# A long convolution by FFT on one core: last stage by row groups in turn, sixteen spectrum buffers, other DRAM copies

## The chip, the core and the metric

The kernel runs on one core of one Trainium2 chip. A core has five engines with their own instruction streams: TensorE (PE in the profile; its weight loads are shown as PEld), VectorE (DVE), ScalarE (ACT), GpSimd (POOL) and SyncE (SP), which here only issues DMAs. They wait for each other through semaphores. The metric is the device time of one execution in microseconds, lower is better. The kernel before was timed three times: 247.57, 248.12 and 249.15 us, median 248.12.

## The reference

Inputs are bf16: `A_u` [1, 2048, 512], parameters of a state-space layer of 512 channels with 128 complex states each, and a small feed-forward network of width 1376.

```python
xn = layernorm(A_u)
K  = real(sum_n C * exp(dt*A*l) * dt*B)            # [512, 2048], one kernel per channel
s  = irfft(rfft(xn padded) * rfft(K padded))[:2048] + xn * Dskip
r  = xn @ B_w_r                                    # one score for each row
i  = argmax(r)                                     # a single row is selected
upd = zero except row i: (silu(xn_i @ w_gate) * (xn_i @ w_up)) @ w_down * sigmoid(r_i)
g  = silu(xn + upd)
out = A_u + s * g
```

So there is one causal convolution of length 2048 in each of 512 channels, whose kernel K must first be generated, and a gate that needs a feed-forward network for one row alone.

## The kernel before

**Where the order comes from.** The Python code records every operation with the buffers that it reads and writes (`_Graph.op`). `schedule` takes a table `ORDER`, written out as numbers of operations, one list for each engine, and `emit` puts each engine's operations out in that order, with the waits that the recorded reads and writes ask for. Each engine is strictly in order; an operation that waits holds up all that follows on its engine, and a DMA that waits holds up SP. Many operations go through helpers, so the profile shows the helper's line: `tt` (two tensors, DVE) is L592, `ts` L599, `cp` L602, `act` L586, `evac` (out of PSUM) L620 on ACT or L621 on DVE, `evac_a` L624, `mm` L641, `dma` L658. Groups are told apart by their buffers.

**The stages, in the order of the data.**

1. Load and layer norm: `X0` to `XN` (bf16, [4 column groups q, 2, 16 rows b, 64]); row l = 16p + b lies on partition p. XN is moved to `XZN` by 16 DMAs, four of its rows to `X4`, and it is stored to DRAM twice, as `scr_x` and `scr_g`, by one DMA of 2 MB each.
2. Router and feed-forward network: a score for each row (`JNK`, L785), argmax through small PE and DVE steps, weights through a ring of eight buffers `WRING` of which five lie where XN was. The result is a row `GRW`, which POOL scatters into `scr_g` at the place that `SMI` names.
3. `useq`, `useq2`: the forward transform of xn, PE `CB,XZN` to `AU` and `AU,F2U` to `UST`, stored as `scr_u` (eight stores).
4. The kernel generator, once for each half h of the channels: exponentials `E` on ACT (`exps`), a chain of complex products on DVE for `GG` (`kgen_g`, buffers TT, MB) and `Q` (`kgen_q`), then 512 small matmuls `QQ,GG` (`kgen_mm`: eight operations of 64) whose results `KE` are sorted by `kx` into `KX[h]`. GG and E are single buffers, used by both halves.
5. `spec(h)`: 16 positions kp, each 10 matmuls `KX,FD` of 128x256 into bank 5 or 6, evicted to a buffer `KF`, which DVE multiplies into `UU[h]` (the product U*KF). `FD` (5 MB) comes in four loads into the space of AU. `UU[0]` lies where the first half's Q was, the first part of `UU[1]` where MB was, its second part where the second half's Q was; each is 4 MB and read back from `scr_u` by `load_u`, in two portions of positions.
6. `inv_a(h)`: 16 operations of eight matmuls `CB,UU`, evicted to `C`. Each needs all 16 products of that half.
7. `fpre`: on DVE and ACT, XNR = xn * Dskip * silu(gate) and XR = A_u + XNR, where XNR is read back from `scr_x`, the gate G0 from `scr_g`, XR from A_u.
8. `fin`, the last stage: 512 matmuls `C,FB`, each 32x32 weights with 128 columns, tile position (32q, 32a). Four blocks bb of four rows for each of the 16 row classes a; a block has four PSUM banks, one for each q. A block's operations are one for each q: 32 matmuls, all in row group q, the column group a running fastest. In block 3 a matmul `VM,CB` (with E127, four partitions) first puts a correction into each bank. Evictions: q even by ACT, then a product with G0 on DVE; q odd by a DVE product straight out of PSUM; then a sum into XR and stores to `out`.

In the table of before, PE has spec0 spread between the second half's QQ,GG operations, its kx1 and, at the end, spec1 with inv0; only three KF buffers serve both halves in turn. The last stage's operations for different q stand one after another.

Of the kernel before, what the change touches and what calls it, by code (L numbers as in the profile page):

```python
# [7 lines left out]
ACT = mybir.ActivationFunctionType  # L8
# [8 lines left out]
KB = 1024  # L17
# [323 lines left out]
def tables():  # L341
# [16 lines left out]
    for l in range(2044):  # L358
# [18 lines left out]
        7 223 8 16 3 9 225 221 12-13 15 17 14 174 110-111 109 107-108 104-106 175 173 167-168 166 169-170 172 171 179 176 178 177 233 231 235 227 229  # L377
        237 239 241 243 245 247 249 251 259 261 263 265 267 269 271 273 343 350 694 357 364 695 275 277 279 371 378 287 700 699 698 385 696-697 392
        784 787 703 702 701 882 789 785 879 786 788 878 871 876-877 880 870 883 881 873-875 872 921-922 920 923 940-941 939 938 956-959 978-979
        982-983""",  # L380
    scalar="""
        2 4 6 10 5 11 18-19 21 20 22-23 28 30 29 31 43 482 468 476 466 477 471 393 474 492 485 26 484 472 496 486 490 473 475 45 487 495 479 489 494
        470 480 491 478 95 465 467 35 469 483 493 394 464 156 481 395 47 443 433 444 396 451 449 437 457 460 434 397 448 436 459 399 458 442 452-453
        456 435 407 462 49 439 406 404 461 441 412 432 446 398 445 290-291 417 413 297 296 293-294 419 418 299-300 302-303 424 306 309 416 311 438 308
        422 312 282 425 463 314-315 317-318 321 320 323-324 440 450 330 326-327 329 455 454 332-333 335-336 526 341-342 447 338-339 537 348 346 345
        349 353 355-356 352 362 257 360 363 359 549 606 609 600 547 366-367 578 607 553 369 373 597 604 596 374 581 595 370 582 594 377 376 605 599
        593 590 598 584 603 583 608 592 580 591 561 588-589 602 579 587 577 586 559 585 383-384 567 380-381 569 388 390-391 575 387 565 563 573 571
        650 640 708 705 711 714 720 668 717 670 726 723 674 732 678 680 682 692 688 738 741 747 750 755 800 803 753 757 806 809 897 885 889 827 893
        765 775 836 773 779 783 839 843 847 853 851 857 855 861 859 865 863 869 867 915 910 933 928 951 946 973 968 981 980 984-985""",
    vector="""  # L390
        1 220 0 54-57 64 114 113 65 112 115 63 51 123 27 25 52-53 117 24 60 59 120 119 61 118 121 50 116 58 62 126 66 124-125 68 67 122 70 69 127 89
        128 71 93 130 72 34 94 33 32 36 132 129 91 39 131 151 133 90 134 150 135 155 136 37 137 154 138 40 86 92 87-88 139 102 97 140 101 103 100 141
        98 152 181 142 99 143 96 183 144 38 145 180 146 185 147 182 148 41 149 153 187 157 401 161 163 165 162 405 159-160 164 158 403 184 189 400 186
        191 188 498 193 409 408 190 195 192 414 194 411 196 497 197 402 198 415 200 420 202 500 499 203 501 204 410 205 502 421 207 503 305 209 505
        211 504 210 212 423 506-507 426 509 508 429 511 214 510 427 219 513 512 428 515 514 283 517 516 284 519 518 529 520-521 528 523 527 522 530
        525 531 524 254 533 532 536 253 535 256 534 255 539 258 541 538 540 542-543 639 545 544 551 611 610 649 613 557 555 281 651 641 285-286 614
        612 616 615 618 617 620 619 621-626 576 627-630 632 631 642 634 633 644 636 635 706 637-638 643 712 646 645 652 648 647 654 653 664 656 655
        709 657-658 721 660 659 666 662 661 718 715 672 727 724 733 676 729 684 730 686 693 690 901 735 904 736 905 739 903 902 742 744-745 748 751
        791 794-795 792 797-798 801 804 759 807 810 763 812-813 815-816 767 818 821 819 822 824 761 825 828 830 771 831 833-834 769 837 777 781 841
        845 849 888 884 890 886 891 887 892 896 894 916 911 895 917 912 898 918 934 919 935 913 929 914 930-931 936 932 937 952 949 947 953 948 950  # L400
        954 971 955 899 969 972 970 974 976 975 977""",
    gpsimd="""
        431 488 430 73-85 601 288""",
    tensor="""
        42 44 46 48 289 295 292 199 201 298 301 206 304 208 307 310 213 313 316 215-218 319 322 222 224 226 328 325 228 230 232 234 331 334 236 238
# [4 lines left out]
        944 943 960 964 963 967 945 961 965""",  # L410
# [7 lines left out]
def build(nc, A_u, A_A_re, A_A_im, A_B_re, A_B_im, A_C_re, A_C_im, A_log_dt, A_Dskip,  # L418
# [22 lines left out]
    p_ = np.arange(128)  # L441
    lidxb = 128.0 * p_[:, None] + np.arange(16)[None, :] + 16384.0
# [6 lines left out]
    cf_list = [("PRMF", perm), ("ONES", ones), ("LIDX", lidxb), ("MISC", misc)]  # L449
# [18 lines left out]
    SCRX = nc.dram_tensor("scr_x", [128 * 8192], BF16)  # L468
    SCRG = nc.dram_tensor("scr_g", [128 * 8192], BF16)

    with g.ctx:
# [76 lines left out]
        XNR = g.buf("XNR", RA, [4, 2, 16, 64], BF16)  # L548
# [13 lines left out]
        KF = [g.buf(f"KF{i}", RT + 9 * KB + 1024 * i, [4, 128], BF16) for i in range(3)]  # L562
# [5 lines left out]
        TB = [g.buf(f"TB{i}", RG + 16 * KB + 1024 * i, [512], BF16) for i in range(3)]  # L568
        V4 = g.buf("V4", RG + 19 * KB, [512], BF16)
# [244 lines left out]
        tt(DV, sml(8, 0, 8), sml(5, 0, 8), CF(CF.a[m0 + 1:m0 + 2], 0, 8), ALU.add)  # L814
# [37 lines left out]
        for fc in range(11):  # L852
# [18 lines left out]
             r=[GRW(None, 0, 8), SMI(None, 0, 8)], cost=1400, dma=16 * KB, tokr=["scrg"], tokw=["row"])  # L871
# [204 lines left out]
        def load_u(h, c):  # L1076
            g.stage = f"ldu{h}"
            uu = UU[h]
            toks = [f"scru{kp}" for kp in range(4 * c, 4 * c + 4)]
            base = 8192 * h + 16 * c * 64  # L1080
            for p0, s0, n in ((0, 0, 128), (0, 64, 64), (64, 0, 64)):
                g.stage = f"ldu{h}" if n == 128 else f"ldv{h}"
                dst = uu(uu.a[0 if n == 128 else 1][:, 16 * c:16 * c + 16].reshape(4, 1024), p0, n)
                load(dst, dram(SCRU, s0 * 16384 + base, [[16384, n], [2048, 4], [1, 1024]]), n * 8192, tokr=toks)
# [164 lines left out]
```

## Time and profile before

| | |
|---|---|
| median of three runs | 248.12 us |
| the profiled execution: its own time | 246.94 us |
| its span, first to last instruction | 244.9 us |
| mean granted TensorE clock | 0.826 |
| busy: PE, DVE, ACT, POOL | 169.0, 194.8, 139.8, 8.2 us |
| DMA moved | 43.27 MB, mean 177 GB/s |
| `C,FB` matmuls (last stage) | 512, 211.5 to 236.7 us |
| `CB,UU` matmuls (inv_a) | 256, 170.2 to 210.5 us |

The profile gives, for one execution, the busy time of each engine, the span cut into 40 slices of 6.1 us (one digit of tenths each), the chain of work that ended last (followed back from the last instruction through what released each step), groups of instructions, and DMA issues. "issue" in the chain is time in which an engine waited for nothing that the profile shows. Durations of matmuls hold their pipeline latency, so a count of starts in a stretch says more of the pace than a mean duration does. On DVE and ACT an instruction starts some 0.08 us before the one ahead of it is recorded as ended; "net" below is a duration less this.

### The profile page before, as it was taken

What the parts mean: (1) busy time and instruction counts of PE and PEld (TensorE: products, weight loads), DVE (VectorE), ACT (ScalarE), POOL (GpSimd) and SP (SyncE); (2) the same over time, 40 slices, a digit from 0 to 9 for tenths busy, and PEclk for the clock granted to TensorE, in tenths of its full rate; (3) what the DMA queues carried; (4) which work ended last, traced back from release to release, by engine and by line L of the source; (5) the groups of instructions that cost most, each with busy time, mean ns of one, the idle gap of its engine ahead of it and who ended that gap; (6) DMA issues with size and microseconds to landing.
All of it is one profiled execution on the core that took longest, in us unless ns stands there. A gap on an engine that the chain in (4) does not pass through costs nothing.

```text
span 244.9 us, 6504 instructions
## 1 busy us (share of the span) xinstructions
PE 169.0 (69%) x2790; PEld 128.3 (52%) x2790; DVE 194.8 (80%) x399; ACT 139.8 (57%) x278; POOL 8.2 (3%) x22
## 2 busy tenths in 40 slices
PE   0330000599887669787646369999999999899970
PEld 0220000374754356655425248878999999665430
DVE  4799999998999995599999943478779649777335
ACT  2699999997997679993420014232488526410200
POOL 2008000000000000010000000000000000000000
PEclk9999999999755577996895757979999999955555
DMA  6980099991766978479989900599999940003306
GB/s 221 329 347 1 0 143 142 301 431 29 229 202 194 278 210 304 130 164 321 398 257 237 236 26 7 125 219 213 229 217 246 214 110 0 3 3 86 90 3 171
DMA packets 26204, 43.27 MB, mean 177 GB/s; under 512 B 2144, under 2 KB 18240, under 8 KB 25280
## 3 DMA queue, kind: packets, MB, share of 16 engines
q1 hardware_dynamic: 24704, 42.01, 64.2%
q10 hardware_dynamic: 1440, 0.85, 1.2%
q8 instruction: 22, 0.36, 0.6%
q14 instruction: 6, 0.05, 0.1%
q0 software_dynamic: 32, 0.00, 0.0%
HBM read 30.26 MB, written 10.49 MB: 166 GB/s over the span
## 4 chain that ended last, share of the span: by engine, by line
PE 52%; DVE 27%; ACT 7%; issue 5%; DMA 3%; POOL 2%; SPq 1%; DVEq 0%
PE PB L641 52%; DVE TT L592 6%; DVE JNK L785 4%; DVE QQ L592 3%; DMA X<-in_A_u_dram 3%; ACT AU L620 3%; DVE GG L592 3%; ACT UST L624 2%; DVE ST L735 2%; DVE XN L599 2%; POOL LST L592 2%; ACT QQ L586 1%; DVE XR L592 1%; DVE TB L592 1%; DVE SL L592 1%
## 5 line engine op out<-in xcount | busy, mean ns | idle before, releaser
L641 PE MATMUL PB<-KX,FD 128*128 128x256 bf16 x320 | 43.5, 298 | 7.9 <-ACT KF L620 6.9
L641 PEld LDWEIGHTS PB<-KX,FD 128*128 128x128 bf16 x320 | 32.8, 107 | 16.1 <-ACT KF L620 8.5
L641 PE MATMUL PB<-QQ,GG 128*20 128x42 bf16 x1024 | 25.0, 263 | 8.6 <-issue 5.5
L592 DVE TENSOR_TENSOR UU<-UU,KF 128x1024 bf16<-128x1024 bf16 x32 | 21.6, 687 | 9.9 <-ACT KF L620 9.5
L641 PEld LDWEIGHTS PB<-QQ,GG 128*20 128x20 bf16 x1024 | 21.9, 123 | 12.2 <-issue 7.3
L641 PE MATMUL PB<-CB,UU 128*128 128x128 bf16 x256 | 26.3, 255 | 0.1
L641 PEld LDWEIGHTS PB<-CB,UU 128*128 128x128 bf16 x256 | 24.9, 201 | 1.4 <-DVE C L621 0.4
L641 PE MATMUL PB<-C,FB 32*32 32x128 bf16 x512 | 23.7, 388 | 0.7 <-ACT C L620 0.7
L592 DVE TENSOR_TENSOR TT<-GG,MB 128x2048 bf16<-128x2048 bf16 (+2 forms) x24 | 23.1, 994 | 0.1
L641 PE MATMUL PB<-CB,XZN 32*128 32x64 bf16 x256 | 14.1, 327 | 13.0 <-DMA XZN<-XN 10.5
L620 ACT ACTIVATE KF<-PB 128x512 bf16<-128x512 f32 x19 | 11.1, 596 | 18.5 <-PE PB L641 13.7
L586 ACT ACTIVATE E<-AR 128x256 bf16<-128x256 f32 x64 | 21.6, 419 | 0.0
L641 PEld LDWEIGHTS PB<-CB,XZN 32*128 32x128 bf16 x256 | 12.1, 201 | 15.0 <-DMA XZN<-XN 10.7
L592 DVE TENSOR_TENSOR QQ<-QQ,E 128x1024 bf16<-128x1024 bf16 (+2 forms) x16 | 19.8, 1254 | 0.0
L620 ACT ACTIVATE C<-PB 128x512 bf16<-128x512 f32 x21 | 12.6, 598 | 12.3 <-PE PB L641 11.3
L624 ACT ACTIVATE UST<-PB 128x512 bf16<-128x512 f32 x32 | 17.3, 602 | 3.8 <-PE PB L641 3.7
L641 PEld LDWEIGHTS PB<-C,FB 32*32 32x32 bf16 x512 | 13.2, 113 | 10.6 <-issue 1.7
L641 PE MATMUL PB<-AU,F2U 64*128 64x256 bf16 x128 | 13.5, 361 | 7.0 <-ACT UST L624 3.9
L586 ACT ACTIVATE TB<-PB 128x512 bf16<-128x512 f32 x8 | 4.7, 596 | 22.7 <-PE PB L641 12.7
L620 ACT ACTIVATE AU<-PB 128x512 bf16<-128x512 f32 x31 | 16.6, 646 | 1.6 <-PE PB L641 1.6
L620 ACT ACTIVATE KE<-PB 128x336 bf16<-128x336 f32 x9 | 4.0, 449 | 22.4 <-PE PB L641 22.4
L592 DVE TENSOR_TENSOR GG<-TT 128x1024 bf16<-128x1024 bf16 (+2 forms) x28 | 14.0, 532 | 1.7 <-PE PB L641 1.5
(120 smaller groups left out, 264.5 us busy)
## 6 DMA issues: line engine op xcount, KB each, us to landing
FD<-c_fd SPq DMA_DIRECT2D x4, 1280.0 KB, 10.1
scr_u<-UST SPq DMA_DIRECT2D x8, 512.0 KB, 5.8
UU<-scr_u SPq DMA_DIRECT2D x8, 512.0 KB, 10.9
UU<-scr_u SPq DMA_DIRECT2D x4, 1024.0 KB, 9.8
X<-in_A_u_dram SPq DMA_DIRECT2D x4, 512.0 KB, 8.3
XZN<-XN SPq DMA_DIRECT2D x16, 128.0 KB, 4.0
scr_g<-XN SPq DMA_DIRECT2D x1, 2048.0 KB, 9.0
scr_x<-XN SPq DMA_DIRECT2D x1, 2048.0 KB, 13.6
```

What stands on the lines that cost most here:

```text
L586: g.op(AC, lambda e: e.activation(out=out.ap, in_=in_.ap, func=func, **kw), w=[out], r=r, cost=cost(AC, out, 0.71) + (92 if bias is not No ...
L592: g.op(eng, lambda e: e.tensor_tensor(out=out.ap, in0=a.ap, in1=b.ap, op=op), w=[out], r=[a, b], cost=cost(eng, out, rate))
L599: g.op(eng, lambda e: e.tensor_scalar(out=out.ap, in0=a.ap, scalar1=x1, scalar2=x2, op0=op0, **kw), w=[out], r=r, cost=cost(eng, out, rate))
L620: g.op(AC, lambda e: e.activation(out=out.ap, in_=in_.ap, func=ACT.Copy), w=[out], r=[in_], cost=cost(AC, out, 0.71), alt=(DV, lambda e: e ...
L624: g.op(AC, lambda e: e.activation(out=out.ap, in_=in_.ap, func=ACT.Copy), w=[out], r=[in_], cost=cost(AC, out, 0.71))
L641: ins = e.matmul(o_.ap, lhsT=l_.ap, rhs=r_.ap, start=st, stop=sp, **kw)
L735: g.op(DV, lambda e, b=b: e.bn_stats(ST6(ST6.a[b]).ap, X0(X0.a[b]).ap), w=[ST6(ST6.a[b])], r=[X0(X0.a[b])], cost=620)
L785: g.op(DV, lambda e, b=b, ro=ro, jk=jk: e.tensor_tensor_reduce(out=jk(jk.a.reshape(8, 64)).ap, in0=xb(XN, b).ap, in1=WRB(WRB.a.reshape(8, ...
```

## The change

- The last stage: one operation holds one row class b4 of a block, 32 matmuls in which the row group q runs fastest, so that neighbours differ in q; it writes four banks. The last block is cut into two of two rows. The correction matmuls are eight, of two rows each (128x256), instead of four. PSUM is evicted in pairs of q: the pair 0,1 by two ACT copies and one DVE product of 1024 elements for each partition, the pair 2,3 by two DVE products from PSUM; then one DVE sum for each pair. `TB` are four buffers of 1024 elements.
- KF: 16 buffers; spec0 uses one for each position, spec1 five of them. KF0 to KF2 lie where they were, KF3 to KF7 behind KX, KF8 to KF15 in the space of E.
- `load_u`: one load for the first part of UU[h] (all positions), two for the second, with 16 KB in one piece for each partition. All wait for all of `scr_u`.
- `scr_x` and `scr_g` are stored by four DMAs each in the row order of the last stage, and A_u is copied inside DRAM to `scr_a` in that order, so that G0, XR and XNR are read back by one, one and two loads instead of four each. The scatter index is worked out for the new order (two more DVE operations, one matmul of 128x8).
- XNR lies in two pieces, one over KE and XN, one over TT and KF0 to KF2. `fpre` works on pairs of q: 24 DVE products and sums of 1024 elements for each partition instead of 12 of 2048.

A new `ORDER` goes with it. In the new table:

- SP issues the copy to `scr_a` after the first weights and before the X4 and XZN moves; the last two FD loads come before the UU[0] loads, then stand: first part of UU[1], GRW, one half of XNR, DSK, second part of UU[1], G0, XR, FB, other half of XNR.
- PE has all 16 positions of spec0 together, ahead of the second half's QQ,GG; inv0 starts between these and kx1, spec1 comes after kx1.
- DVE evicts seven of the first half's eight KE operations (ACT did five of them before) and takes all but one of the 16 products of spec0 after the second half's Q; ACT's exponentials of the second half stand earlier, among the evictions to UST.
- In the last stage PE has: one operation of block 0, the four of block 1, then the other three of block 0 with the corrections of block 3 between them, block 3, block 2, the corrections of block 4, block 4.

The diff without the table:

```diff
+    addrb = 128.0 * (32 * (p_[:, None] % 4) + p_[:, None] // 4) + np.arange(16)[None, :]
...
+    SCRA = nc.dram_tensor("scr_a", [128 * 8192], BF16)
...
-        XNR = g.buf("XNR", RA, [4, 2, 16, 64], BF16)
+        XNR = apart("XNR", RX + 8 * KB, RT + 4 * KB, [2, 2, 16, 64])
...
-        KF = [g.buf(f"KF{i}", RT + 9 * KB + 1024 * i, [4, 128], BF16) for i in range(3)]
+        KF = [g.buf(f"KF{i}", RT + 9 * KB + 1024 * i if i < 3 else RQ0 + 37 * KB + 1024 * (i - 3) if i < 8 else RM + 1024 * i, [4, 128], BF16) for i in range(16)]
...
         for t, nm in ((SCRX, "scrx"), (SCRG, "scrg")):
-            store(t.ap().rearrange("(p f) -> p f", p=128), XN(XN.a.reshape(-1)), 128 * 16384, tokw=[nm])
+            for a in range(4):
+                dma(dram(t, 262144 * a, [[8192, 32], [1, 8192]]), bass.AP(tensor=XN.handle, offset=a * XN.row, ap=[[4 * XN.row, 32], [1, 8192]]), 32 * 16384, r=[XN(XN.a.reshape(-1))], tokw=[f"{nm}{a}"])
+        g.stage = "cpa"
+        dma(dram(SCRA, 0, [[8192, 32], [262144, 4], [1, 8192]]), _dma_rows(A_u, 0, [[32768, 32], [8192, 4], [1, 8192]]), 128 * 16384, tokw=["scra"])
...
-        tt(DV, sml(8, 0, 8), sml(5, 0, 8), CF(CF.a[m0 + 1:m0 + 2], 0, 8), ALU.add)
+        tt(DV, LST(LST.a[7]), oneh, cf("ADDR"), ALU.mult)
+        red(sml(9), LST(LST.a[7]), ALU.add)
+        mm([(mv(134, 1, 0, 8), cf("ONE8"), sml(9), True, True, None)], 300)
+        tt(DV, sml(8, 0, 8), mv(134, 1, 0, 8), CF(CF.a[m0 + 1:m0 + 2], 0, 8), ALU.add)
...
+        def load_u(h):
+            uu = UU[h]
+            toks = [f"scru{kp}" for kp in range(8)]
+            load(uu(uu.a[0].reshape(8192)), dram(SCRU, 8192 * h, [[16384, 128], [1, 8192]]), 128 * 16384, tokr=toks)
+            for i in range(2):
+                load(uu(uu.a[1].reshape(8192), 64 * i, 64), dram(SCRU, 8192 * h + (1 - i) * 64 * 16384, [[16384, 64], [1, 8192]]), 64 * 16384, tokr=toks)
...
-                kf = KF[n_ % 3]
+                kf = KF[3 + n_ % 5 if h else n_]
...
+        for qp in range(2):
+            load(XNR(XNR.a[qp].reshape(-1)), dram(SCRX, 4096 * qp, [[8192, 128], [1, 4096]]), 128 * 8192, tokr=[f"scrx{a}" for a in range(4)])
+        load(G0(G0.a.reshape(-1)), dram(SCRG, 0, [[8192, 128], [1, 8192]]), 128 * 16384, tokr=[f"scrg{a}" for a in range(4)] + ["row"])
+        load(XR(XR.a.reshape(-1)), dram(SCRA, 0, [[8192, 128], [1, 8192]]), 128 * 16384, tokr=["scra"])
...
+        for kb, (r0, nr) in enumerate(((0, 4), (4, 4), (8, 4), (12, 2), (14, 2))):
+            bk = [PB[4 * (kb % 2) + q] for q in range(4)]
+            if r0 >= 12:
                 for q in range(4):
-                    mm([(bk[q](bk[q].a.reshape(4, 128)), CB(cb("E127"), 0, 4), VM(VM.a[:, 128 * q:128 * q + 128], 0, 4), True, None, None)], 215)
-            for q in range(4):
+                    mm([(bk[q](bk[q].a[0:128 * nr].reshape(nr, 128)), CB(cb("E127"), 0, 4), VM(VM.a[r0 - 12:r0 - 12 + nr, 128 * q:128 * q + 128], 0, 4), True, None, None)], 215)
+            for b4 in range(nr):
                 lst = []
-                for b4 in range(4):
-                    for ri in range(2):
-                        for a in range(4):
-                            l1 = 16 * a + 4 * bb + b4
+                for ri in range(2):
+                    for a in range(4):
+                        l1 = 16 * a + r0 + b4
+                        for q in range(4):
                             lst.append((bk[q](bk[q].a[128 * b4:128 * b4 + 128].reshape(2, 64), 32 * a, 32), FB(FB.a[l1, ri], 32 * q, 32),
...
                 mm(lst, 28)
...
+                for q in range(2):
+                    if qp:
+                        tt(DV, t_(t_.a[128 * nr * q:128 * nr * (q + 1)].reshape(2, nr, 64)), cols(2 * qp + q), G0(G0.a[2 * qp + q, :, r0:r0 + nr]), ALU.mult)
+                    else:
+                        act(t_(t_.a[128 * nr * q:128 * nr * (q + 1)].reshape(2, nr, 64)), cols(2 * qp + q), ACT.Copy)
+                if not qp:
+                    tt(DV, tv(0, 2), tv(0, 2), gv(0, 2), ALU.mult)
+                xv = XR(XR.a[r0:r0 + nr, 256 * qp:256 * qp + 256].reshape(nr, 4, 64).transpose(1, 0, 2))
+                tt(DV, xv, t_(t_.a[0:256 * nr].reshape(4, nr, 64)), xv, ALU.add)
```

More of the change, by code (lines that the diff above doesn't have):

```diff
@@ L384 @@
[L384 to L387, printed above, removed]
@@ L411 @@
+        963-964 944-947 979 976-978 980-981""",
 )
@@ L567, in build @@
         XR = g.buf("XR", RG, [16, 512], BF16)
-        TB = [g.buf(f"TB{i}", RG + 16 * KB + 1024 * i, [512], BF16) for i in range(3)]
-        V4 = g.buf("V4", RG + 19 * KB, [512], BF16)
+        TB = [g.buf(f"TB{i}", RG + 16 * KB + 2048 * i if i < 2 else RQ0 + 33 * KB + 2048 * i, [1024], BF16) for i in range(4)]
+        V4 = g.buf("V4", RQ1 + 41 * KB, [512], BF16)
         FIX = {DV: 62.0, AC: 118.0, PO: 250.0}
@@ L870, in build @@
         g.op(PO, lambda e: e.indirect_dma_start(out=rows, out_offset=bass.IndirectOffsetOnAxis(ap=SMI(None, 0, 8).ap, axis=0), in_=GRW(None, 0, 8).ap, in_offset=None),
-             r=[GRW(None, 0, 8), SMI(None, 0, 8)], cost=1400, dma=16 * KB, tokr=["scrg"], tokw=["row"])
+             r=[GRW(None, 0, 8), SMI(None, 0, 8)], cost=1400, dma=16 * KB, tokr=[f"scrg{a}" for a in range(4)], tokw=["row"])
         g.stage = "useq"
@@ L1073, in build @@
             kgen_mm(h)
-        def load_u(h, c):
+        def load_u(h):
+            uu = UU[h]
+            toks = [f"scru{kp}" for kp in range(8)]
             g.stage = f"ldu{h}"
[L1078 to L1084, printed above, removed]
+            load(uu(uu.a[0].reshape(8192)), dram(SCRU, 8192 * h, [[16384, 128], [1, 8192]]), 128 * 16384, tokr=toks)
+            g.stage = f"ldv{h}"
+            for i in range(2):
+                load(uu(uu.a[1].reshape(8192), 64 * i, 64), dram(SCRU, 8192 * h + (1 - i) * 64 * 16384, [[16384, 64], [1, 8192]]), 64 * 16384, tokr=toks)
         def load_fd(buf, i, k0):
@@ L1196, in build @@
+            for a in range(4):
+                store(_dma_rows(out, 8192 * a + 512 * r0, [[32768, 32], [1, 512 * nr]]), XR(XR.a[r0:r0 + nr].reshape(-1), 32 * a, 32), 32 * 1024 * nr, eng=SP if r0 < 12 or a < 2 else AC)
         g.schedule(ORDER)
```

106 lines of the change are left out of this document (46 added, 60 removed), and 7 rows, old and new, of the table tensor.

## The prediction

> **What bounds the kernel now.** I read the busy slices first, then the chain that ended last in order of time, then stretches of the last third. In the slices, VectorE (DVE) is full to about slice 23 and TensorE (PE) from slice 25 on; in the last five slices the granted clock is half.
>
> ```profile
> PE   0330000599887669787646369999999999899970
> ...
> DVE  4799999998999995599999943478779649777335
> ...
> PEclk9999999999755577996895757979999999955555
> ```
>
> The chain says the same: up to 136 us DVE (the generators), then PE with small gaps, then 25.6 us of the last stage, then a tail on DVE.
>
> ```profile
> 136.64 1.25 PE PB L641 x43
> 137.89 4.27 issue
> ...
> 149.28 46.61 PE PB L641 x578
> ...
> 211.48 25.59 PE PB L641 x464
> 237.16 0.69 DVE TB L592
> ```
>
> So two things are for sale: when DVE lets PE start its long run, and the pace of the last stage. For the pace I cut four slots of 0.22 us out of it (columns: PE, weight loads PEld, DVE, ACT, POOL, each busy us and count, then clock, DMA share, GB/s):
>
> ```profile
> 212.54:212.76 0.22, 0.22 (x16) 0.12 (x8) 0.20 (x1) 0.00 (x0) 0.00 (x0) 1.00 0.00 0
> 212.76:212.98 0.22, 0.22 (x16) 0.12 (x8) 0.00 (x0) 0.00 (x0) 0.00 (x0) 1.00 0.00 0
> 225.17:225.39 0.22, 0.22 (x8) 0.13 (x4) 0.22 (x2) 0.00 (x0) 0.00 (x0) 0.50 1.05 335
> 225.39:225.61 0.22, 0.22 (x8) 0.13 (x4) 0.22 (x2) 0.00 (x0) 0.00 (x0) 0.50 1.12 261
> ```
>
> PEld is the column to read: four weight loads, one for each column group, start per 0.22 us while one operation on one row group runs; at 212.5, where two operations on different row groups overlap, it is eight. One row group thus goes round load, multiply, load at 0.22 us per four matmuls whether the clock reads 1.00 or 0.50, and two groups do so side by side.
>
> **The change, part by part.** All times are of the profiled execution (span 244.9 us).
>
> *Start.* The copy of A_u inside DRAM (2 MB read, 2 MB written) is queued on SP ahead of the X4 and XZN moves. In 18 to 30 us the stretch row shows 2 GB/s: an empty 12 us. The nearest rows are the 2 MB stores scr_g (9.0 us) and scr_x (13.6 us), so it costs 0 to 1.6 us; I take 0, since the nearer ends fit. If the cover goes, XZN, the "useq" matmuls and everything after are late one for one. Six more stores of XN (0.64 us of SP each, 3.9 us) end before the ring loads that wait for XN anyway (59.7 us). The router gains two small DVE operations (0.08 us net each) and one PE round trip before SMI, which only the scatter needs: between 0 and 1 us, I take 0.2.
>
> *Generators on DVE.* The second half's GG may be written when PE has read the first: 104.2 us now. DVE sat idle 13.1 of those us, 5.3 of them after 92 us, waiting for PE and for KE evictions queued on ACT behind exponentials. The new table gives seven of eight to DVE. From the end of the first half's Q (94.4 now, 95.2 with ACT's share moved to DVE) four operations of 64 at 1.5 us remain: 101.4, gain 2.8. In the new order 35.9 us of DVE rows stand between there and the last product of the second half's Q (37.1 before, with four spectrum multiplies in between, now one): 137.3, against 142.4. A risk sits on ACT: exponentials of the second half wait for E, with U evictions behind them. By my reading PE's last first-half operation still comes at 99.7 to 101; bound 0 to 3 us.
>
> *Sixteen KF buffers.* All 160 spec0 matmuls now stand ahead of the second half's QQ,GG. Ten positions run while DVE works; KF8 to KF15 lie on E, so ACT waits for the last product with E (about 123 us), then six positions at 1.25 us: done near 133, before Q needs PE. What is late next is DVE: the 15 remaining products U*KF (0.61 us net) and two KE evictions (0.43), 137.3+10.0 = 147.3. Only then can inv0 start.
>
> *U by halves.* The first product now needs all of U0 (4 MB) where it needed 2 MB. It is issued when the last scr_u store has landed (about 115), after the FD loads. The row 103 to 120 us moves 263 GB/s, 155 to 180 moves 214: 15 to 19 us, landing 130 to 135, against a first use at 136. The price is nothing, but the cover is 1 to 6 us thin; beyond, one for one.
>
> *The long PE run.* From 147.3: inv0 16 x 0.86, one QQ,GG operation 1.5, kx1 5.2 (3.9 of it matmuls, the rest its evictions), spec1 16 x 1.10, inv1 16 x 0.88: 52.1 us, plus 3 for waits and the slow clock at the start (0.61 in 136 to 149, 0.88 to 165): 202.4, against 211.5 now. Beside it DVE has uum1 (9.8), eight KF evictions (4.9) and the prologue "fpre", 24 products of 1024 where 12 of 2048 stood: 24 x 0.61 = 14.6 us, as before. SP holds XNR[1] until KF0 to KF2 are read (146.5), then DSK, U1's second part, G0, XR and FB until the QQ,GG operations end (about 151): 9 MB, at 214 GB/s to 189 us. By that rate U1 lands at 161 (first used, by the walk above, at 166), G0 at 170 (175), XR at 180 (184), XNR[0] at 189 (190). At the old rate it just fits; 0 to 4 us, I take 0 as the 3 above covers one miss.
>
> *The last stage.* Its 512 matmuls now go through the four row groups in turn. If all four groups turn at 0.22 us, 16 per turn, 512 cost 7.0 us; at the two-group pace 14. No row has four groups; the fastest long run is this, 22 ns each:
>
> ```profile
> 151.91 2.81 PE L641 MATMUL PB<-QQ,GG 128*20 128x42 bf16 x128
> ```
>
> I take 22 ns: 0.7 us for one row of 32, 11.2 in all. The Trainium skill, page "TensorE: Matmul & The Clock Gate", Part 3, says that weight loads overlap a running matmul only where the row group differs, which the 0.22 us slots agree with. Its Part 1 gives a floor near 25 ns between starts; by it the 512 would take 12.8 us and the sum 1.6 more. The 22 ns row speaks against.
>
> Evictions then set the end. Per block of four rows DVE has two products out of PSUM (0.61), one product (0.61) and two sums (0.61): 3.05; the two half blocks 1.7 each; 12.5 in all, as before (13.0). Walked through in the new order from the stage's start: block 0's first row 0.7, block 1 to 3.5, then block 0's rows between the E127 matmuls. Each of these broke the stream by 0.9 us (from 222.8 to 223.67 around one VM matmul); there are four breaks, and block 3 ends at 9.7. Block 2 waits for block 0's last bank, 9.3 by DVE, and ends at 12.5. DVE frees its banks by 14.0; E127 and two rows to 16.3; DVE's last five, 2.0: 18.5. Now it is 30.4 (211.5 to 241.9). Bounds: 15 (7.0 us of matmuls, cheaper breaks) to 30.4.
>
> *Sum.* 202.4 + 0.7 (the idle before the stage now) + 18.5 + 3.0 (last DVE to end of span, now) = 224.6. The profiled execution took 246.94, 2.0 over its span: 226.6. The median shown, 248.12, is 1.2 above it: **228**.
>
> **Rivals.**
> *Two groups at a time.* PE issues matmuls too slowly to keep four groups turning: eight in 0.22 us as at 212.5, 27 ns each, 14.0 us instead of 11.2: 231. For: it is the best that this stage shows. Against: the 22 ns row. Chance 0.14. The floor of Part 1 of the page named above points to this rival.
> *The last stage keeps its pace* because of its breaks and bank waits: 30.4 instead of 18.5, 240. For: 0.9 us breaks, twice as many E127 matmuls, DVE's 12.5 us. Against: block 0's rows fill the waits. Chance 0.12.
> *Nothing is gained ahead of 211.5*, the last stage is: 237. For: in 136 to 149 PE lost 4.27 us to "issue" while it waited for nothing else, which a new order need not avoid; ACT's wait on E; the thin covers of the loads. Against: spec0's multiplies stood in PE's way until 169.5. Chance 0.18.
> *Slower: U0 lands late.* DVE takes the first U product in order ahead of the last two of Q, so a late U0 stops DVE, then mm11, then all of PE. Price: one for one past 136 us. It outweighs the 20 us gained from a landing at 156 on: 4 MB in 41 us, 98 GB/s, which is the rate of 136 to 149 (97), where little was asked for; 103 to 136 shows 263. From 251 up. Chance 0.09, with the copy at the start as a helper.
> *The gains cancel* (late loads eat the last stage's): 246 to 250, chance 0.05.
> The forecast itself has 0.42.
>
> **Numbers.** About 1% is what a measurement of this kernel can tell from no change. Faster by more: forecast, two groups, kept pace and no early gain, 0.42 + 0.14 + 0.12 + 0.18 = 0.86; within: 0.05; slower: 0.09. The range goes down to 219 (last stage at 15, a full clock in the long run, -3.5 and -5) and up to 241, past the kept pace; outside are the last two rivals and small tails.
>
> **What would show it.** Right: in the last stage about 16 weight loads or more per 0.35 us, and the stage from its first C,FB matmul to the last DVE operation in 17 to 20 us; the first CB,UU matmul at 146 to 150 (170.2 now); 160 KX,FD matmuls ahead of the second half's QQ,GG; inv1 ending near 203. Wrong: DVE idle before the first U product with the UU loads as releaser; ACT idle before KF8 for longer than 10 us; PE "issue" idle of several us; or a last stage in which PE waits for evictions more than it computes.

## The result and the profile after

The changed kernel takes **226.13 us** (median of four runs, 224.92 to 227.20) against 248.27 us for the kernel before (four runs, 247.57 to 249.15): a ratio of 0.9105, 95% interval 0.905 to 0.9161. The profiled execution took 227.2 us, its span is 225.4 us. With each experiment below stand its median and, in brackets, its ratio to the kernel before, timed beside it, with the 95% interval. The medians are of all executions; the ratios leave out slow ones, over 1.5% above the fastest of the same kernel, of which e2, e8, e11 and e12 have some.

The busy slices of the changed kernel (slices of 5.6 us; PE, VectorE, granted clock):

```profile
PE   0303010078968658895999794276999999998760
...
DVE  3899999989899999853979999697386999980993
...
PEclk9999999999995555998899998858879999999955
```

PE is full from slice 29 (158 us) on, where before it was full from slice 25 (147 us) on, but the stretch is shorter, and the five slices at half the clock at the end have become two. In the hole in PE's row at slices 25 and 26 (135 to 147 us, where before had the digits 3 and 6) spec0 is done, and PE waits for Q and then for KE evictions that stand behind products of U and KF on DVE. The chain that ended last, in order of time (start, length, what), from the first half's QQ,GG on:

```profile
99.15 2.32 PE PB L643 x99
101.47 2.69 issue
104.16 6.03 PE PB L643 x65
...
111.81 7.71 DMA scr_u<-UST
...
120.50 21.45 DMA UU<-scr_u
141.95 1.94 issue
143.89 0.69 DVE UU L594
...
155.27 16.61 PE PB L643 x226
...
205.80 2.48 PE PB L643 x140
...
221.14 0.42 DVE XR L594
```

Two things differ from the chain of before. PE stops for 2.69 us at 101.47 and waits for nothing that the profile shows; before had such a stop at this place too, but a shorter one:

```profile
102.04 1.26 issue
103.30 0.91 PE PB L641 x30
```

And the chain goes through the store of scr_u and the load of U0 instead of through DVE. The 1.94 us that are called "issue" at 141.95 are U0 too: in the trace DVE's wait ahead of the first product ends at 143.85, and the last count of one of U0's loads comes at 143.81. The landmarks against the forecast's, in us of the profiled executions:

| | forecast | before | after |
|---|---|---|---|
| second half's GG first written | 101.4 | 104.2 | 104.9 |
| second half's Q done | 137.3 | 142.4 | 145.3 |
| first CB,UU matmul | 147.3 | 170.2 | 155.3 |
| first C,FB matmul | 203.1 | 211.5 | 205.8 |
| last DVE operation ends | 221.6 | 241.9 | 221.6 |
| end of the span | 224.6 | 244.9 | 225.4 |

So of the 19.5 us of span, 14.7 come from the last stage (30.4 to 15.8 us from its first matmul to DVE's last end), 5.7 from an earlier start of it, and the tail gave back 0.8. Three slots of 0.44 us in that stage (busy us and count of PE, weight loads PEld, DVE, ACT, POOL, then clock, DMA share, GB/s; an instruction that is under way at the edge of a slot is counted too):

```profile
206.66:207.10 0.44, 0.44 (x56) 0.43 (x35) 0.00 (x0) 0.00 (x0) 0.00 (x0) 1.00 0.00 0
207.10:207.54 0.44, 0.44 (x56) 0.44 (x36) 0.00 (x0) 0.00 (x0) 0.00 (x0) 1.00 0.00 0
218.30:218.74 0.44, 0.44 (x38) 0.35 (x37) 0.44 (x2) 0.00 (x0) 0.00 (x0) 0.50 0.91 270
```

An operation of 32 matmuls takes 0.44 us, 13.7 ns for one with its weight load, and it does so at a granted clock of 1.00 and of 0.50 alike. In the kernel before, the operations of 32 start 0.9 to 1.7 us apart where no correction stands between them.

### The profile page after: what moved, and what is told of

Read it like the earlier page. It is cut to its first block, busy times and chain, and to the rows that moved or that the text cites. A ratio compares the mean times of both kernels' runs of the same rounds, so it can differ in the third digit from the quotient of the medians.

```text
span 225.4 us, 6510 instructions
## 1 busy us (share of the span) xinstructions
PE 151.0 (67%) x2796; PEld 120.5 (53%) x2796; DVE 190.2 (84%) x397; ACT 146.0 (65%) x289; POOL 7.5 (3%) x22
## 4 chain that ended last, share of the span: by engine, by line
DVE 35%; PE 32%; DMA 16%; ACT 8%; issue 4%; POOL 2%; SPq 1%
PE PB L643 32%; DMA UU<-scr_u 10%; DVE TT L594 5%; DVE UU L594 5%; DVE QQ L594 5%; DMA scr_u<-UST 3%; DVE JNK L790 3%; DMA X<-in_A_u_dram 3%; DVE ST L737 3%; DVE TB L594 2%; ACT AU L622 2%; ACT QQ L588 2%; ACT SL L588 2%; DVE XN L601 2%; DVE XR L594 2%
## 5 line engine op out<-in xcount | busy, mean ns | idle before, releaser
L643 PE MATMUL PB<-KX,FD 128*128 128x256 bf16 x320 | 36.6, 273 | 1.7 <-ACT KF L622 1.4
L643 PEld LDWEIGHTS PB<-KX,FD 128*128 128x128 bf16 x320 | 30.7, 98 | 6.6 <-ACT KF L622 2.2
L643 PE MATMUL PB<-QQ,GG 128*20 128x42 bf16 x1024 | 23.1, 262 | 14.5 <-DVE QQ L594 5.8
L643 PE MATMUL PB<-CB,UU 128*128 128x128 bf16 x256 | 27.4, 265 | 1.8 <-DVE UU L594 1.8
L622 ACT ACTIVATE KF<-PB 128x512 bf16<-128x512 f32 x24 | 14.1, 596 | 17.8 <-PE PB L643 15.7
L594 DVE TENSOR_TENSOR UU<-UU,KF 128x1024 bf16<-128x1024 bf16 x32 | 20.5, 690 | 3.9 <-issue 1.9
L626 ACT ACTIVATE UST<-PB 128x512 bf16<-128x512 f32 x32 | 17.2, 606 | 3.3 <-PE PB L643 3.2
L622 ACT ACTIVATE C<-PB 128x512 bf16<-128x512 f32 x23 | 13.8, 598 | 6.0 <-PE PB L643 5.1
L643 PE MATMUL PB<-CF,PAR 128*128 128x128 f32 x16 | 4.1, 439 | 18.5 <-DVE LST L740 9.9
L643 PEld LDWEIGHTS PB<-CB,XZN 32*128 32x128 bf16 x256 | 12.3, 201 | 7.0 <-ACT AU L622 6.2
L594 DVE TENSOR_TENSOR GG<-TT 128x1024 bf16<-128x1024 bf16 (+2 forms) x28 | 13.9, 528 | 2.2 <-PE PB L643 2.1
L643 PEld LDWEIGHTS PB<-CF,PAR 128*128 128x128 f32 x16 | 3.6, 328 | 18.7 <-ACT PAR L712 10.2
L737 DVE BATCH_NORM_STATS2 ST<-X 128x6 f32<-128x512 bf16 x16 | 10.3, 677 | 3.4 <-DMA X<-in_A_u_dram 3.4
## 6 DMA issues: line engine op xcount, KB each, us to landing
UU<-scr_u SPq DMA_DIRECT2D x2, 2048.0 KB, 14.7
```

What stands on the lines that cost most here:

```text
L594: g.op(eng, lambda e: e.tensor_tensor(out=out.ap, in0=a.ap, in1=b.ap, op=op), w=[out], r=[a, b], cost=cost(eng, out, rate))
L622: g.op(AC, lambda e: e.activation(out=out.ap, in_=in_.ap, func=ACT.Copy), w=[out], r=[in_], cost=cost(AC, out, 0.71), alt=(DV, lambda e: e ...
L626: g.op(AC, lambda e: e.activation(out=out.ap, in_=in_.ap, func=ACT.Copy), w=[out], r=[in_], cost=cost(AC, out, 0.71))
L643: ins = e.matmul(o_.ap, lhsT=l_.ap, rhs=r_.ap, start=st, stop=sp, **kw)
L737: g.op(DV, lambda e, b=b: e.bn_stats(ST6(ST6.a[b]).ap, X0(X0.a[b]).ap), w=[ST6(ST6.a[b])], r=[X0(X0.a[b])], cost=620)
```

## The experiments

### The order of the matmuls, done alone and undone alone

e1 is the kernel before with the alternation only; the blocks stand in plain order:

```diff
-            for q in range(4):
-                lst = []
-                for b4 in range(4):
-                    for ri in range(2):
-                        for a in range(4):
+            for b4 in range(4):
+                lst = []
+                for ri in range(2):
+                    for a in range(4):
+                        for q in range(4):
...
-    908 906 909 942 924 926 925 907 927 962 966 944 943 960 964 963 967 945 961 965
+    906-909 924-927 942-945 960-967
```

> The kernel before, with one part of the change alone: an operation of the last stage holds one row of a block with the row group running fastest (32 matmuls in four banks), and the blocks stand in plain order. All else is as before. Forecast's theory (the pace of the matmuls was the bound of that stage, and evictions come next): 512 matmuls take 7 to 9 us instead of 25.6, DVE's 13 us of evictions and the 4.9 us of leftover prologue on DVE (211.5 to 217.1) set the end; the stage goes from 30.4 us to 18 to 20, so 236 to 238 us. Rival (the old eviction by q and the in-order blocks hold the stage, and the new pairing of evictions is what made it short): no better than 243.

Measured: 236.72 us against 247.82 (0.9577, 0.950 to 0.9655), 11.1 us less; the stage takes 19.6 us from its first matmul to DVE's last end. The matmuls of the last stage in e1 (busy us, mean ns, then idle before and what ended it):

```profile
L640 PE MATMUL PB<-C,FB 32*32 32x128 bf16 x512 | 8.2, 379 | 5.4 <-DVE TB L591 3.3 <-issue 1.4 <-ACT C L619 0.7
```

PE now waits 3.3 us for evictions where it had waited for none, and DVE's waits in the stage fall from 12.3 us (7.2 for PE, 5.1 for ACT) to 1.7: for most of the stage the bound went from the matmuls to DVE, as forecast.

e5 undoes the same thing alone in the changed kernel: the list of a block is made with q outermost and cut into the same operations of 32.

```diff
-            for b4 in range(nr):
-                lst = []
-                for ri in range(2):
-                    for a in range(4):
-                        for q in range(4):
+            for q in range(4):
+                for b4 in range(nr):
+                    for ri in range(2):
+                        for a in range(4):
```

> The changed kernel with the old order of the matmuls in the last stage: all of a block's matmuls of row group 0, then of group 1, 2 and 3, cut into the same operations of 32; nothing else is undone (pairs of q in the evictions, blocks, order, buffers). By the row of before (25.6 us for the 512) an operation takes 1.3 to 1.7 us instead of 0.44 and the stage 25 to 27 us instead of 15.8: 235 to 237 us. Rival (as with eight of one row group in a row, 0.59 us per operation, evictions cover it): 226 to 228.

Measured: 233.99 us (0.9419, 0.9339 to 0.9498), 7.9 us more than the changed kernel; the stage takes 24.5 us, a little under the 25 to 27 that were expected. Its group row:

```profile
L643 PE MATMUL PB<-C,FB 32*32 32x128 bf16 x512 | 19.7, 386 | 0.7 <-ACT C L622 0.7
```

PE is busy for 19.7 us with them and, after the start, waits only 0.9 us ahead of a correction: the matmuls are the bound again. So the alternation is worth 8 to 11 us of the 22. The rest lies ahead of the stage and in what else was changed in it (pairs of evictions, blocks, less of the prologue beside it), which no run takes apart.

### What in the order counts

Both kernels are the changed one, with only the loops inside an operation exchanged.

```diff
 # e2: eight matmuls of one row group, then of the next
+                for q in range(4):
                     for ri in range(2):
                         for a in range(4):
-                            for q in range(4):
 # e3: column group slowest, row group fastest
+                for a in range(4):
                     for ri in range(2):
-                        for a in range(4):
                             for q in range(4):
```

> The changed kernel, with the 32 matmuls of an operation of the last stage in another order: eight of row group 0, then eight of group 1, and so on. A 32x32 tile of the array seems to take one matmul per 0.22 us: in the changed kernel 16 different tiles start within 0.11 us and then PE waits for the turn to end. Here four tiles are asked for twice running: about 0.97 us per operation instead of 0.44, 15.5 us for the 512, stage from 15.8 us to 19 to 20.5, so 229.5 to 231. Rival (evictions on DVE set the end whatever the order): within 1 us of the changed kernel, 225 to 227.

> The changed kernel, with the column group slowest in an operation of the last stage: four matmuls of the four row groups on one column group, the same four tiles again for the imaginary part, then the next column group. Neighbours always differ in their row group. Theory of the tiles (each 32x32 tile takes one matmul per 0.22 us, whatever its neighbours): as with eight of one row group in a row, 0.97 us per operation, 229.5 to 231. Rival (what matters is that neighbours differ in row group, so that a weight load can run beside the matmul ahead): 0.44 us per operation, no change, 225 to 227.

Measured: 224.94 us (0.9059, 0.8996 to 0.9123) and 227.04 us (0.9161, 0.9112 to 0.921); neither can be told from the changed kernel. In both an operation takes 0.58 to 0.59 us (starts of the weight loads 32 apart): not the 0.97 of the theory of the tiles, and in e3 not the 0.44 of the rival either. Both lose 0.15 us for each of 16 operations, 2.4 us in all; evictions cover part of it, and the stage of e3 lasts 17.2 us against 15.8. The Trainium skill, page "TensorE: Matmul & The Clock Gate", Part 3, says that a weight load overlaps a running matmul only where the row group differs. In e3 neighbours always differ in it, as in the changed kernel, and the pace is another; so that rule alone does not give it. That a turn through all 16 tiles before any comes again is the fastest of the four orders seen (0.44; 0.58 twice; 0.9 to 1.5 us in e5) is shown; why is open.

### U0's landing and the order of DVE

e4 takes two causes of the late start away: DVE finishes Q before it asks for U0, and ACT evicts two KE operations that stood among DVE's products.

```diff
-    vector: ... 667 670 669 734 672 671 737 755 749 678 722 676 740 ...
+    vector: ... 667 670 669 672 671 734 737 755 749 722 740 ...
-    scalar: ... 754 674 682 ...
+    scalar: ... 754 674 676 678 682 ...
```

> The changed kernel with two moves in the order: DVE finishes the second half's Q before the first product of spec0, which waits for U0; and the two evictions of KE that stood among the products on DVE go to ACT, which is idle there. Theory (start of the long run is set by DVE: U0's late landing costs it 1.9 us, of which 0.9 can be filled with the last two operations of Q, and 0.8 are the evictions): first CB,UU matmul 1.7 to 2.5 us earlier than in the changed kernel (155.3 there), end 223.5 to 224.5. Rival (the next wait takes it: U1 lands when it did, and DVE waited 1.9 us for it already): first CB,UU earlier, but the end within 0.5 us of the changed kernel.

Measured: 223.45 us (0.9039, 0.8986 to 0.9092). The median is 2.7 us lower, the intervals overlap. The first CB,UU matmul comes at 151.1, the C,FB stage starts at 201.3 (205.8). From the first write of GG to the first CB,UU it is 47.7 us against 50.4. That does not credit the order with 2.7 us: e3 and e5 have the changed kernel's order in this stretch, in their executions DVE did not wait for U0 at all (last counts 137.1 and 139.5), and they took 48.0 and 48.3 us. So the order is worth 0.3 to 0.7 us where U0 comes in time; the rest of the difference is U0, late in one execution and not in the other.

e9 lengthens the wait: U0's loads behind the first part of U1 on SP.

```diff
-    sync: ... 707-708 710 709 791 297 877 ...
+    sync: ... 707 791 297 708 710 709 877 ...
```

> The changed kernel with the loads of U0 issued behind the first part of U1 and GRW on SP, so that they start when DVE has read MB for the last time (near 132.6 us) instead of when scr_u is written (119.5). This lengthens the wait that the forecast called a thin cover. Forecast's rival on the late U0 (one for one past the point at which DVE wants it, and everything behind stops with DVE): the issue comes 13 us later, 2 MB of U1 go first, the landing falls near 151 to 155, the first U product 9 to 13 us later than in the changed kernel and the end as much: 234 to 239 us. Other reading (some of it comes back, since U1 is in place and PE and ACT catch up): end less than 7 us later, under 233.

Measured: 239.09 us (0.9635, 0.959 to 0.9681), 13.0 us more than the changed kernel. The chain of e9:

```profile
134.44 21.46 DMA UU<-scr_u
...
155.98 0.69 DVE UU L594
```

and what DVE waited for:

```profile
DVE UU L594 <- DMA UU<-scr_u: 14.6, 1, 14.6
```

The last of the three loads was issued 13.9 us later than in the changed kernel, the first product comes 12.1 us later and the span is 11.8 us longer. One for one holds.

### Sixteen buffers against eight

e7 is e4 with eight KF buffers, and PE does positions 8 to 15 of spec0 behind the second half's QQ,GG.

```diff
-    kf = KF[3 + n_ % 5 if h else n_]
+    kf = KF[3 + n_ % 5 if h else n_ % 8]
-    tensor: ... 732 729 738 735 744 741 750 747 756 753 673 675 677 681 679 685 683 761 ...
+    tensor: ... 732 729 673 675 677 681 679 685 683 738 735 744 741 750 747 756 753 761 ...
```

> The kernel of e4 with eight KF buffers for spec0 instead of 16: PE has positions 0 to 7 where it had them, positions 8 to 15 behind the second half's QQ,GG and ahead of inv0, since they need the buffers back from DVE's products; the products stand in the order of the positions. Forecast's theory (spec0 ahead of the second half's QQ,GG is what lets inv0 start early): 8 x 1.1 us of PE come into the path ahead of inv0, of which the two last evictions and products add 1.3; against e4 (first CB,UU 9.7 us after Q is done) inv0 starts 5 to 7 us later, end 228 to 231. Rival (the start is set by DVE's 16 products, 9.7 us after Q, and PE's idle time there takes the eight positions): inv0 at most 2 us later than in e4, end 223 to 226.

Measured: 234.05 us (0.9438, 0.935 to 0.9525), 10.6 us more than e4. The chain of e7 after the end of Q:

```profile
140.18 3.34 issue
...
144.82 5.06 PE PB L643 x192
149.88 0.75 issue
150.62 9.61 PE PB L643 x102
...
160.26 0.61 ACT KF L622
...
160.89 0.70 DVE UU L594
```

Of the 9.61 us, 8.9 are the eight positions, each followed by its product on DVE, and inv0 starts at 161.6 (151.1 in e4). The rival, that PE's idle time there would take them, falls: that idle time is 1.8 us in e4. The loss is also more than the 5 to 7 us that the theory gave. The two stretches of "issue" in this chain, 4.1 us, are stops of PE as in the next section; in e4 PE has 1.9 us of them, beside DVE's products, while here all 4.1 lie on the path. By this chain some 6.5 us of the loss are the eight positions and 4.1 the stops; no run takes the two apart.

### PE's stop of 2.7 us

e6 shifts PE's instructions: in an idle stretch at the start an operation repeats its four matmuls 16 times.

```diff
-    ... for q in range(4)], 430 if i < 2 else 110)
+    ... for q in range(4)] * (17 if i == 2 else 1), 430 if i < 2 else 110)
```

> The changed kernel with 64 matmuls more on PE near the start: those of the last parameter transpose are repeated 16 times (same operands, same result) in a stretch in which PE is idle for 13 us. In the changed kernel PE stops for 2.7 us inside the last but one operation of the first half's QQ,GG (matmul 983 of its stream), while a 16 KB packet of the instruction queue is under way; 16 KB are 256 instructions, 128 matmuls with their weight loads. Theory (PE waits for its own instructions there): the stop falls 64 matmuls earlier in the work, in the operation ahead (near 99.8 us by the clock of the changed kernel), or goes away; the packets of the instruction queue shift with it. Rival (something of the work or of the DMA traffic at that time stops PE): it stays in the same operation at the same matmul of it. Time: within 1 us of the changed kernel if the stop moves by one operation, 2 to 3 us less if it goes away.

The timeline of PE in the changed kernel, and then in e6 (start, length, what, count, idle before it):

```profile
99.15 2.32 PE L643 MATMUL PB<-QQ,GG 128*20 128x42 bf16 x104
104.16 0.68 PE L643 MATMUL PB<-QQ,GG 128*20 128x42 bf16 x24 [2.69 <-issue]
```

```profile
101.94 1.01 PE L643 MATMUL PB<-QQ,GG 128*20 128x42 bf16 x40
105.48 1.99 PE L643 MATMUL PB<-QQ,GG 128*20 128x42 bf16 x88 [2.53 <-issue]
```

The stop came after 104 of the last 128 matmuls of this half and comes after 40: exactly 64 earlier. In the ten experiments that keep PE's order up to there it stands at the same matmul as in the changed kernel (behind the 488th QQ,GG), 2.5 to 3.2 us from one start to the next, and in each the trace has a packet of 16 KB on the instruction queue that starts within 0.8 us of the last matmul ahead of the stop and, in the changed kernel, takes 0.9 us.

In the kernel before and in e1, whose PE order is another, the stop (1.5 us) stands behind the 479th QQ,GG. That is the same count from the start of PE's stream: 984 matmuls, in all 14 traces. And in all 14 PE starts again 1.4 to 1.6 us after that packet has ended; in before the packet began 0.9 us ahead of the last matmul, in the changed kernel 0.7 us after it, and the stop is longer by about that. The same holds for every stop of PE of 1 us or more that these traces call "issue", 27 in all: a packet of 16 KB ended 1.3 to 1.6 us ahead of each restart. A stop that goes with the instruction, and not with the work, and that ends with the packet, is PE out of instructions. Why the packet comes later in the changed kernel is open.

The time did not follow the expectation: 228.79 us (0.9229, 0.9135 to 0.9322), 2.7 us more than the changed kernel. In the last stage of e6 PE stops three times on "issue", 2.9 us in all, where the changed kernel has no such stop, and the stage takes 17.0 us instead of 15.8; the stretch from the first CB,UU to it takes 52.2 us instead of 50.5.

### The copy in DRAM

e8 leaves the copy out and reads XR straight from A_u, e10 does so by four DMAs.

```diff
 # e8
-    load(XR(XR.a.reshape(-1)), dram(SCRA, 0, [[8192, 128], [1, 8192]]), ...)
+    load(XR(XR.a.reshape(-1)), _dma_rows(A_u, 0, [[8192, 4], [32768, 32], [1, 8192]]), ...)
 # e10
+    for a in range(4):
+        load(XR(XR.a.reshape(-1), 32 * a, 32), _dma_rows(A_u, 8192 * a, [[32768, 32], [1, 8192]]), ...)
```

> The changed kernel without the copy of A_u inside DRAM at the start (1 KB is copied in its place); XR is read by one DMA straight from A_u, whose rows are taken in the order of the last stage. Forecast's theory (the copy lies in idle DMA time and costs 0): the first XZN matmuls come within 0.5 us of the changed kernel's and the time is within 1 us of it. Rival 1 (the copy delays X4 and XZN and so the forward transform): first XZN matmuls 0.5 to 2 us earlier, time 0.5 to 2 us less. Rival 2 (the copy is what makes XR's load fast): XR's load takes over 2 us longer, and DVE waits for it in the prologue.

> The kernel of e8 (no copy of A_u inside DRAM), with XR loaded straight from A_u by four DMAs of 32 partitions each, one for each row class group, instead of one DMA with three dimensions. Theory (the single DMA with its three dimensions was the slow thing in e8, not the lack of the copy): XR's loads take 10 to 25 us, DVE does not wait for them for more than 2 us, and the time is that of the changed kernel within 1 us (224 to 227). Rival (reading A_u in this order of rows is slow in any form): DVE waits over 10 us for XR and the time is above 236.

Measured: 252.04 us (1.0144, 1.0036 to 1.0252) and 226.32 us (0.9114, 0.9066 to 0.9161). What DVE waited for in e8, and the traffic in that stretch (PE, PEld, DVE, ACT, POOL, clock, DMA share, GB/s):

```profile
DVE XR L594 <- DMA XR<-in_A_u_dram: 27.1, 1, 27.1
```

```profile
190.00:200.00 10.00, 0.00 (x0) 0.00 (x0) 0.00 (x0) 0.00 (x0) 0.00 (x0) 0.51 0.25 67
200.00:210.60 10.60, 0.00 (x0) 0.00 (x0) 0.00 (x0) 0.00 (x0) 0.00 (x0) 0.50 0.24 75
```

One DMA whose outer dimension is 4 keeps a quarter of the 16 DMA engines busy, and the 2 MB land 53 us after their issue. The Trainium skill, page "DMA: Bandwidth & Descriptors", section "Why a DMA increments its semaphore by 16 and not by 1", says that the number of engines is the largest up to 16 that divides the slowest dimension of both patterns; with 4 that is 4 of 16, which the 0.25 agrees with. With four DMAs of 32 rows each DVE does not wait for XR and the time is that of the changed kernel. So the copy costs nothing (the first CB,XZN matmul starts at 44.15 without it, at 44.1 to 45.4 in kernels with it and PE's old start), and it gains nothing over four loads.

### A faster version

e11 is e4 with one more move on PE, and e12 is e11 with blocks 0 and 3 of the last stage evicted by ACT alone.

```diff
-    tensor: ... 681 679 685 683 761 759 687 765 ...
+    tensor: ... 681 679 685 683 687 761 759 765 ...
 # e12 besides
-    if qp:
+    if qp and kb not in (0, 3):
...
```

> The kernel of e4 (Q ahead of the first product, the two KE evictions on ACT) with the last QQ,GG operation of the second half ahead of inv0's first operation: PE stood idle for 1.9 us there, waiting for DVE's last product, and that operation takes 1.3 us. Theory (the long run is bound by PE, so what is taken out of it comes off the end): 1 to 1.9 us less than e4 (223.45), 221.3 to 222.6. Rival (the operation has to wait for its bank and for ACT, and inv0 starts late by as much): within 0.5 us of e4.

> The kernel of e11, and in blocks 0 and 3 of the last stage all four banks are evicted by ACT, so that DVE does one product of SBUF operands there instead of two out of PSUM; blocks 1, 2 and 4 stay. Theory (from the first block on, DVE is busy without a break and sets the end of the stage): 0.95 us less of DVE, 0.6 to 1 us less than e11. Rival (the chain of banks and of the TB buffers sets the end: PE waits 1.6 us for them ahead of block 4): no gain over e11.

Measured: 224.01 us (0.9005, 0.8967 to 0.9043) and 224.79 us (0.9033, 0.8992 to 0.9075). e11's interval lies below the changed kernel's: some 1% faster than it, and 10% faster than the kernel before. Against e4 (223.45) no gain can be told by the total, and the 221.3 to 222.6 of the theory was not reached. In the traces the stretch from the first CB,UU to the first C,FB matmul is 48.3 us (50.2 in e4), near the 1.9 us of the theory, but e12, which has the same move, takes 49.8 there; so the gain is not shown. In e12 the rival holds; what waited in its last stage:

```profile
PE PB L643 <- DVE TB L594: 2.8, 1, 2.8
DVE TB L594 <- ACT TB L588: 2.6, 1, 2.6
```

ACT takes the four banks of a block one after another, so DVE waits for operands and the banks come free later: the stage takes 17.5 us instead of 15.7.

## Why the prediction came out as it did

The sum was right to 0.8 us of span (224.6 against 225.4) and the median lay 1.9 us below the 228, inside the range. Its terms were less good than the sum: against the forecast inv0 started 8.0 us late, the long run gave back 5.3 and the last stage 2.7, so the close agreement is luck. Of the signs of being right that it named, the pace of the weight loads and the place of the 160 KX,FD matmuls came; the stage was to take 17 to 20 us (15.8), the first CB,UU matmul to come at 146 to 150 (155.3) and inv1 to end near 203 (205.1). Two signs of being wrong came too: DVE idle 1.9 us for U0, and a PE "issue" idle of 2.7 us.

*The copy at the start: 0.* Right (e8, e10).

*GG can be written at 101.4.* Wrong: 104.9, and 102.7 to 105.8 in e3 to e5 and e7 to e12, which have this order. The forecast let PE's last first-half operation come at 99.7 to 101 with a bound of 3 us; it began at 100.5, and PE then stood without instructions for 2.7 us (e6). The 1.26 us of "issue" at 102.04 in the trace of before are the same stop, and the forecast had no term for it. The 4.27 us of "issue" at 137.89 are of that kind too, with a packet of the instruction queue at 139.6 and PE's restart 1.4 us after its end; the forecast used them as an argument for a rival and not as a term of the sum.

*35.9 us of DVE from there to Q.* 40.4 in the profiled execution: 1.9 of it U0, 1.4 a wait for the feed-forward result on PE that had no term, and 1.2 a sum that was too small.

*U0 issued at 115 and landed by 130 to 135.* Wrong on both: issued at 119.5 to 120.5, since PE's stop held back the last transform and its eviction and the last store then took 7.7 us (the eight have a median of 4.9), and landed at 143.8, 24 us after the first issue where 15 to 19 were taken; at 137.1 and 139.5 in e3 and e5. The cover was not 1 to 6 us but 0.1 to 2.3 us in e3, e5, e6, e8 and e10, and U0 was 1.9 us late in the profiled execution of the changed kernel. The price, one for one, was right (e9). The point from which a late U0 outweighs the gains was set wrong: in e9 it lands at 155.9, just there, and the kernel is still 8.8 us faster than before. DVE asks for U0 at 139 to 143 in the runs just named, not at 136.

*10.0 us from Q to inv0.* Right, 9.9; and that spec0 had to stand ahead of Q for it is shown by e7 (10.6 us, PE's stops included). The 160 KX,FD matmuls ended at 135.2, and ACT's wait for E ahead of KF8 was 2.1 us.

*The long run, 52.1 + 3.* 50.5 us from the first CB,UU to the first C,FB, 50.2 to 52.1 in e3, e4, e5 and e10. The rows hold and the 3 us for waits and the slow clock were not needed: kx1's evictions lie beside inv0's operations, and PE is idle for 0.2 us in 50.

*The last stage, 18.5.* 15.8, near the lower bound of 15. The mechanism was right (e1, e5) and one size was off, 13.7 ns a matmul in place of 22: by the walk block 3 was to end at 9.7 us of the stage and block 2 at 12.5, and they end at 6.7 and 9.8. The four breaks at the E127 matmuls, put at 0.9 us each, cost 0.5 to 1.0. What sets the end is DVE, as forecast: it starts 2.5 us into the stage (3.5 by the walk) and then has 0.4 us idle. The rival of two groups at a time falls with the pace, and so does the floor near 25 ns between starts that the Trainium skill, page "TensorE: Matmul & The Clock Gate", states in Part 1: here 32 take 0.44 us, 16 of them starting within 0.13 us. The rival "nothing is gained ahead of 211.5" adds up to 236 and not to 237, since 211.5 has the idle 0.7 us in it already.

*Tail and offset.* The tail was 3.8 us instead of 3.0; the profiled execution took 1.8 us over its span (2.0 used). The median of the four runs lay 1.1 us below the profiled execution, where 1.2 above had been added as in before: 2.3 us that say nothing of the kernel.

So the start of the last stage came 2.7 us later than forecast, and the stage itself was 2.7 us shorter.

## What to carry to other kernels

Where small matmuls on tiles of the array are the bound, go through all the tiles before one comes again, and then look at what evicts them, since that is the next bound. Give early work its own buffers when the engine that frees the old ones is the busy one: eight more buffers of 1 KB for each partition were worth 10 us here, some 4 of them through stops of PE. When a transfer is said to be hidden, work out its issue time from everything ahead of it on its queue, a stop of PE included; a cover of a few us is no cover.

## What the runs showed of the hardware

- 16 matmuls of 32x32x128 on 16 different tiles, each with its own weight load, start 8 to 9 ns apart; then PE pauses, and the next 16 begin 0.22 us after the first 16 did, at a granted clock of 1.00 and of 0.50 (in e1, at 0.50 from 221.1 us on, operations of 32 start 0.42 to 0.44 us apart).
- PE's instructions come in packets of 16 KB. On a run of matmuls at 22 ns it stood for 1.5 us (before, e1) or 2.5 to 3.2 us (the others), always at the same instruction, and went on 1.4 to 1.6 us after a packet had ended; 64 matmuls more at the start moved the stop 64 matmuls ahead in the work (e6). Whether other DMA traffic (share 0.87 to 1.1 at that moment) makes it longer was not tried.
- While a load of 2 MB whose outer dimension is 4 was under way (e8), the DMA engines moved 67 to 75 GB/s at a share of 0.24 to 0.25; the changed kernel's loads in 161 to 181 us move 304 at 0.98.
